# All units of an attention and maxout kernel queued in another order

## The chip, the cores and the metric

The kernel runs on one core of one Trainium2 chip. The metric is the device time of one execution in microseconds (us): the median of the runs, beside the time of one execution under the profiler.

## The reference

Four sequences of 768 tokens, 8 heads of 64. Each query sees the first 8 positions (at a fixed distance) and the last 96, with a bias that falls with distance at a slope of its own for each head. The heads' outputs stand side by side as 3072 rows of 512 and go through a network whose hidden layer is the maximum of three products.

```python
scores = scale * np.matmul(q, k.transpose(0, 1, 3, 2))
keep = is_global | is_local          # pos < 8, or 0 <= rel < 96
dist = np.where(is_global & ~is_local, float(n_local), np.abs(rel))
scores = np.where(keep, scores - slopes[:, None, None] * dist, -1e9)
a = softmax(scores)                  # over the keys
x = np.matmul(a, v)                  # to (3072, 512)
h = np.maximum(np.maximum(x @ w1, x @ w2), x @ w3)    # 512 -> 768
return h @ w_out                     # 768 -> 512
```

## The kernel before, in words

The work is cut into units, each a small function, and a string SCHEDULE lists 504 of them. A loop at the end of the kernel calls them in that order, and every engine then runs its own instructions strictly in that order: a unit that waits holds all that stands behind it on its engine. SP issues nearly all DMAs, in the same order. Within one unit, TensorE, ACT, VectorE, GpSimd and SP only wait for one another where data or a buffer ties them.

A unit is a letter and numbers. T is a token tile of 128 tokens (0 to 23, six to a sequence), n is a part of two tiles (0 to 11). The last number often names the engine of the copy: 0 ACT, 1 VectorE, 2 GpSimd.

- l n.s loads queries (s = 0) or keys (s = 1) of part n (load_part, tile rawp; l0.1 goes by ACT's queue, the others by SP's), c n.s.how casts them to bf16 (cast_part, tile qkp), x n.s.how transposes them into qkT: on TensorE through PSUM (how 2 and 3 in whole tiles with one copy of 1024 columns; 6, 7, 8 in halves with two copies: one on each engine, both on ACT, both on VectorE), or by a DMA on SP (9).
- v n loads values, C n.e.how casts half of them into vo (the first part of a sequence into vof), Y n.half.how copies rows of vo into ve or vf, which hold the same values at another shift; V T.how and G T.how write the 8 global values and keys in their place, Z b.how gathers the first keys of a sequence into kf.
- B h.how and K h make the bias and the mask of head h from the distances (tiles bias, wmask).
- S T.g.how are the scores of four heads (PSUM tile sp) and their exponential on ACT (tile P). With how 1 the bias is added on TensorE by two matmuls with the identity; with how 0 M T.g multiplies P by wmask on VectorE later.
- A T.how multiplies by the values (PSUM op; with 2, two smaller tiles oph) and normalises on VectorE (tile xb); T T.how transposes the result into xT: on TensorE, copied by ACT (0, 7), VectorE (1, 8) or both (6), or by a DMA on SP (4).
- w, o load weights, W, Q cast them. F c.f.j is one of the three products of hidden block f in chunk c: four matmuls into PSUM h (line 424), then for j = 0 a copy on ACT (429), for j = 1 and 2 a maximum on VectorE (431, 433). Chunks hold 4, 2, 2, 4, 4, 4, 4 token tiles; chunks 1 and 2 are of half width. O c.tt.how is the output of one token tile: six matmuls (439), a copy (448) and a store. E is the last chunk's, in pieces.
- D i.n is n filler matmuls (line 504, tile wp), whose result is not used.

PSUM sets limits to the order: three rotating buffers (h) for F, O, the filler and half the transposes, one buffer (tp) for the other transposes, and two (sp0, sp1) for S and A. Loads have 5 buffers for queries and keys and 3 for values.

Of the kernel before, what the change touches and what calls it, by code (L numbers as in the profile page):

```python
# [22 lines left out]


SCHEDULE = """
    K7 l1.0 c1.0.2 K6 l1.1 B6.1 D0.6 D4.4 B5.1 D2.0 D5.4 K0 c0.1.1 c0.0.1 K2 D8.0 B0.1 B4.0 B1.0
    B3.0 x0.1.3 K1 K3 K5 c1.1.2 B7.0 x0.0.7 D1.1 D9.2 S1.0.1 Z0.1 B2.1 v0 C0.0.2 S1.1.1 G1.0 x1.0.8
    K4 M1.0 S0.0.1 M0.0 v1 x1.1.8 S2.1.1 S2.0.1 M2.0 C0.1.2 Y0.1.2 Y1.0.1 M1.1 V2.1 Y0.0.1 G2.1 A1.2
    S0.1.1 C1.0.2 C1.1.2 Y2.0.0 Y1.1.2 D3.1 S3.0.1 M3.0 M0.1 A0.2 S3.1.1 M3.1 l2.0 c2.0.2 x2.0.6
    T1.1 M2.1 A2.0 V3.2 T0.0 G3.0 A3.1 l2.1 c2.1.2 x2.1.6 T2.1 w0.0 W0.0.0 l3.0 w0.1 S4.0.1 M4.0  # L30
    T3.8 V4.2 W0.1.2 S4.1.0 D7.1 G4.0 w0.2 F0.1.0 F0.0.0 S5.1.0 c3.0.1 x3.0.6 M4.1 w1.0 W1.0.0
    S5.0.0 F0.1.1 W0.2.2 F0.1.2 v2 C2.0.0 C2.1.0 W2.0.1 F0.0.1 F0.0.2 M5.0 F0.3.0 F0.2.0 M5.1 Y2.1.1
    V5.1 F0.5.0 w1.1 W1.1.0 W2.1.1 F0.4.0 A4.1 A5.0 F0.5.1 T4.0 F0.4.1 w1.2 W1.2.0 l3.1 T5.1 F0.2.1
    F0.2.2 l4.0 c4.0.1 W2.2.0 F0.5.2 c3.1.0 x3.1.7 Z1.0 F0.4.2 F1.0.0 F1.2.0 l4.1 c4.1.1 S7.0.0
    S6.1.0 l5.0 x4.0.6 l5.1 o0 F1.0.1 F1.0.2 c5.0.1 M7.0 F1.3.0 F1.4.0 F1.4.1 o2 c5.1.1 x4.1.7
    S6.0.0 S7.1.0 G7.0 v3 F1.2.1 F1.2.2 F1.3.1 Q2.1 F0.3.1 M7.1 Q0.0 F1.5.0 F1.5.1 S8.0.0 x5.0.7
    S8.1.0 G8.1 C3.0.2 C3.1.1 Y4.0.1 F0.3.2 F1.5.2 A7.0 F1.4.2 F1.1.0 M6.0 x5.1.6 v5 o1 Q1.0 v4
    S9.0.0 S9.1.0 l7.0 l6.1 C5.0.1 C5.1.0 F1.1.1 F1.3.2 Y3.1.1 M8.0 F1.1.2 T7.0 v6 l6.0 M6.1 v7
    Y3.0.1 M9.0 O0.2.1 l7.1 C4.0.0 O0.0.0 G9.0 V8.1 A6.1 c7.0.1 M8.1 c6.1.1 x6.1.9 O0.3.0 C4.1.0
    Y4.1.1 O0.1.1 Y5.1.0 S10.1.0 T6.8 V9.1 M9.1 S10.0.0 O1.0.0 A8.1 M10.1 T8.4 F2.0.0 x7.0.9 G10.0  # L40
    F2.4.0 c6.0.0 l8.1 v9 l9.1 F2.0.1 F2.1.0 M10.0 F2.0.2 S11.0.0 c7.1.0 Y5.0.1 x6.0.6 S11.1.0 V10.1
    F2.1.1 M11.0 F2.4.1 C6.0.0 A9.0 F2.2.0 V11.1 l9.0 O1.1.1 S13.1.0 x7.1.6 S13.0.0 G13.0 M11.1
    F2.2.1 F2.1.2 C6.1.1 F2.2.2 A11.1 F2.3.0 F2.5.0 A10.0 Y6.1.0 Z2.0 F2.4.2 T11.0 F2.5.1 F2.3.1
    C7.0.0 S12.1.0 T9.8 S12.0.0 F2.3.2 v8 C7.1.1 F2.5.2 M12.0 S14.1.0 T10.6 S14.0.0 c8.1.0 O2.0.0
    l8.0 M13.0 G14.1 Y7.1.1 M12.1 F3.2.0 V15.0 M13.1 c9.1.1 x9.1.9 F3.0.0 Y7.0.1 A13.1 F3.3.0 l11.1
    T13.4 M14.0 x8.1.9 M14.1 F3.0.1 S15.1.0 Y6.0.0 S15.0.0 F3.3.1 F3.3.2 F3.1.0 M15.0 M15.1 V14.0
    F3.4.0 c8.0.1 c9.0.0 x9.0.9 l10.0 F3.0.2 A12.1 F3.2.1 x8.0.9 C9.0.0 C8.0.0 A14.0 F3.1.1 T12.4
    l10.1 G15.1 Y8.0.1 c11.1.0 O2.1.0 A15.1 F3.5.0 F3.1.2 C9.1.1 F3.2.2 T15.8 S19.0.0 M19.0 S19.1.0
    c10.0.0 T14.4 C8.1.0 Y8.1.0 F3.4.1 l11.0 v10 F3.5.1 F3.5.2 F3.4.2 Y10.0.1 M19.1 Z3.1 S16.0.0
    S16.1.0 G16.1 V20.0 O3.3.0 O3.2.1 A19.1 F4.5.0 c10.1.1 x10.1.9 v11 F4.1.0 V16.1 G19.1 x10.0.9  # L50
    Y9.0.1 S18.1.0 S17.0.0 M17.0 M16.1 F4.3.0 F4.3.1 F4.5.1 M16.0 V17.1 F4.1.1 S17.1.0 S18.0.0
    F4.2.0 Y9.1.0 O3.0.0 M18.0 M17.1 C10.0.1 M18.1 A16.1 F4.1.2 T19.4 O3.1.1 A18.0 A17.1 C11.0.1
    c11.0.0 x11.0.9 F4.0.0 F4.2.1 F4.2.2 F4.3.2 T18.4 S20.1.0 S20.0.0 T16.4 T17.4 x11.1.9 C10.1.1
    Y10.1.1 F4.0.1 G20.1 F4.0.2 F4.5.2 S21.0.0 S21.1.0 G21.0 M20.0 F4.4.0 F4.4.1 C11.1.1 F4.4.2
    M21.1 F5.1.0 F5.2.0 V21.1 O4.2.1 F5.3.0 Y11.1.0 F5.3.1 M20.1 S22.0.0 S22.1.0 F5.2.1 F5.5.0
    Y11.0.0 F5.2.2 V23.1 F5.4.0 A20.1 F5.3.2 M22.0 M21.0 G22.0 S23.0.0 M23.0 S23.1.0 T20.4 F5.5.1
    O4.1.1 A21.1 T21.4 M23.1 M22.1 O4.0.0 V22.0 F5.4.1 F5.0.0 A23.1 T23.4 O4.3.0 A22.0 F5.4.2 F5.5.2
    F5.0.1 F5.1.1 F5.0.2 T22.4 F5.1.2 F6.3.0 F6.5.0 F6.4.0 F6.5.1 F6.4.1 F6.4.2 O5.1.0 F6.3.1 F6.1.0
    O5.3.1 F6.1.1 F6.0.0 F6.0.1 F6.0.2 O5.0.1 F6.2.0 F6.2.1 F6.3.2 O5.2.0 F6.2.2 F6.1.2 F6.5.2 E
    D6.0  # L60
"""


# [510 lines left out]
```

## Time and profile before

| | us |
|---|---|
| median of 3 runs | 176.2 (176.19 to 176.25) |
| the profiled execution, its own time | 176.69 |
| span of that execution in the trace | 174.9 |
| TensorE busy | 168.4 |
| VectorE busy | 133.0 |
| ACT busy | 120.1 |
| GpSimd busy | 14.0 |

The times of rows are those of the profiled execution, from the start of its span. A timeline row gives start, length, engine, line, operation, tiles and count, and in brackets how long the engine was idle and what ended that. Where a row merges several instructions, its length runs from the first start to the last end; spacings of starts are shorter than lengths, since the instructions of an engine overlap a little. A line number is that of the kernel before; the changed kernel's lines from 57 on are one lower, because its SCHEDULE has one line less.

### The profile page before, as it was taken

The numbers are of one execution on the slowest core, as the hardware profiler recorded it, in microseconds if no ns is written. First come the engines' busy times: TensorE is split into PE (matmuls) and PEld (weight loads), VectorE is DVE, ScalarE is ACT, GpSimd is POOL, SyncE is SP. The second block draws the span as 40 slices with busy tenths as digits, with TensorE's granted clock in tenths as the row PEclk, the third lists the DMA queues.
The fourth block names the chain that finished last, engine by engine and source line by source line (L and its number), as shares of the span: only waits on it lengthen the run. The fifth ranks groups of instructions, "written<-read, shape, count | busy, mean of one in ns | idle before, by whom it ended". The sixth has DMA issues, their size and how long they took to land.

```text
span 174.9 us, 4215 instructions
## 1 busy us (share of the span) xinstructions
PE 168.4 (96%) x1664; PEld 92.8 (53%) x1685; DVE 133.0 (76%) x287; ACT 120.1 (69%) x188; POOL 14.0 (8%) x25
## 2 busy tenths in 40 slices
...
GB/s 130 350 301 334 363 350 381 384 335 325 317 275 278 324 280 223 291 219 211 219 226 216 285 208 177 166 133 60 56 8 30 108 168 0 0 119 36 88 27 213
DMA packets 55508, 35.92 MB, mean 205 GB/s; under 512 B 18369, under 2 KB 47937, under 8 KB 55489
## 3 DMA queue, kind: packets, MB, share of 16 engines
...
q8 instruction: 13, 0.21, 0.5%
...
## 4 chain that ended last, share of the span: by engine, by line
PE 88%; ACT 5%; DVE 3%; issue 2%; POOL 1%; POOLq 0%; ACTq 0%
PE h L424 52%; PE po L439 18%; PE sp L306 7%; PE op L360 5%; ACT wmask L326 2%; PE tpr L261 2%; PE sp L299 2%; ACT bias L322 1%; ACT qkT L268 1%; PE xtp L411 1%; ACT P L317 1%; POOL qkp L188 1%; PE oph L360 1%; PE xtr L401 0%; DVE xb L373 0%
## 5 line engine op out<-in xcount | busy, mean ns | idle before, releaser
L424 PE MATMUL h<-xT,w 128*128 128x512 bf16 (+1 forms) x489 | 99.5, 348 | 0.9 <-issue 0.3
L424 PEld LDWEIGHTS <-w 128*128 128x128 bf16 x504 | 46.6, 98 | 41.0 <-ACT w L493 1.1
L317 ACT ACTIVATE P<-sp 128x1024 bf16<-128x1024 f32 (+1 forms) x48 | 44.0, 956 | 9.2 <-PE sp L306 9.1
L429 ACT CAST h<-h 128x512 bf16<-128x512 f32 (+1 forms) x42 | 21.8, 531 | 21.9 <-PE h L424 21.8
L439 PE MATMUL po<-wo,ht 128*128 128x512 bf16 (+2 forms) x150 | 33.8, 362 | 0.4
L431 DVE TENSOR_TENSOR h<-h,h 128x512 bf16<-128x512 bf16 (+1 forms) x42 | 25.2, 605 | 10.9 <-PE h L424 8.9
L433 DVE TENSOR_TENSOR ht<-h,h 128x512 bf16<-128x512 bf16 (+1 forms) x42 | 25.5, 608 | 6.7 <-PE h L424 5.0
L334 DVE TENSOR_TENSOR P<-P,wmask 128x1024 bf16<-128x1024 bf16 x33 | 22.4, 696 | 2.0 <-ACT P L317 1.9
L439 PEld LDWEIGHTS <-ht 128*128 128x128 bf16 x156 | 14.4, 98 | 15.0 <-DVE ht L433 0.2
L448 ACT COPY ost<-po 128x512 f32<-128x512 f32 (+2 forms) x16 | 8.8, 554 | 15.8 <-PE po L439 15.3
L373 DVE TENSOR_TENSOR xb<-op,rz 128x512 bf16<-128x512 f32 x22 | 15.2, 692 | 0.8
L360 PEld LDWEIGHTS <-P 128*128 128x128 bf16 x352 | 13.4, 97 | 4.0 <-issue 0.2
L306 PE MATMUL sp<-qkT 64*128 64x128 bf16 x320 | 14.3, 217 | 0.2
L306 PEld LDWEIGHTS <-qkT 64*128 64x128 bf16 x320 | 9.3, 94 | 8.4 <-issue 5.1
L448 DVE COPY ost<-po 128x512 f32<-128x512 f32 (+1 forms) x10 | 6.5, 648 | 8.4 <-PE po L439 8.4
L188 DVE CAST qkp<-rawp 128x1024 bf16<-128x1024 f32 x12 | 8.2, 687 | 2.0 <-DMA rawp<-in_k_dram 1.8
L188 ACT CAST qkp<-rawp 128x1024 bf16<-128x1024 f32 x8 | 8.4, 1050 | 0.0
L504 PE MATMUL wp<-const-bfloat16-1.0 128*128 128x512 bf16 x19 | 7.5, 539 | 0.9 <-PEq L555 0.8
L268 ACT COPY qkT<-tpr 128x512 bf16<-128x512 bf16 x12 | 6.6, 588 | 1.0 <-PE tpr L261 1.0
L268 DVE COPY qkT<-tpr 128x512 bf16<-128x512 bf16 x6 | 4.0, 688 | 3.6 <-PE tpr L261 3.6
L261 PE MATMUL tpr<-identb,qkp 64*128 64x64 bf16 x208 | 5.4, 190 | 0.6 <-DVE qkp L188 0.2
L493 ACT CAST w<-wst 128x1024 bf16<-128x1024 f32 x5 | 5.1, 1047 | 1.0 <-DMA wst<-in_moe_w_dram 1.0
...
## 6 DMA issues: line engine op xcount, KB each, us to landing
...
```

The lines of the kernel that those rows point to most:

```text
L188: copies[how](qk, src)
L306: nc.tensor.matmul(sp[:, z, i, ds], k_cols(T, hsl, jp, ds), q_cols(T, hsl, jp), start=not how, stop=True, skip_group_check=True)
L317: nc.scalar.activation(dst, src, AF.Exp, bias=0.0, scale=scale)
L334: nc.vector.tensor_mul(P, P, wmask[:, g, :, 0:2])
L360: nc.tensor.matmul(o, P[:, i, ds], vs[ds][:, h], start=(ds == 0), stop=(ds == len(vs) - 1), skip_group_check=True)
L373: nc.vector.tensor_tensor(out=x.rearrange("p (g h) d -> p g h d", g=2), in0=o4[:, :, :, 0:64], in1=rz[:, :, :, None].to_broadcast([128, 2, ...
L424: nc.tensor.matmul(ps, w123[f // 2][:, dm, j, (f % 2) * 128:(f % 2) * 128 + 128], xT[c][:, dm], start=(dm == order[0]), stop=(dm == order[ ...
L429: nc.scalar.copy(h01, ps)
L431: nc.vector.tensor_max(h01s[c, f], h01s[c, f], ps)
L433: nc.vector.tensor_max(ht[c][:, f], h01s[c, f], ps)
L439: nc.tensor.matmul(po, ht[c][:, f, tt * 128:(tt + 1) * 128], wo[:, f, cols], start=(f == 0), stop=(f == NF - 1))
L448: copy(ost, po)
```

## The change

Only SCHEDULE differs: 500 units instead of 504, all in another order, and for many the engine of a copy. Work is the same but for this: S4.0 takes mask M4.0 and no bias matmuls; A16 and A20 are split in two PSUM tiles; T9 and T15 go by DMA; x3.1 and x1.1 are transposed in whole tiles now, x0.1 in halves; ten D units have become six, and the filler is 19 matmuls in both, of which one (D9.1) now stands behind E. Summed over the program the ACT copies of O go from 11 to 16, the VectorE casts c from 12 to 15, the GpSimd casts C from 5 to 2 (C0.0, C0.1 and C1.0 go to VectorE, Y0.0 and V2 to GpSimd). The first line of the string, before and now, and the units up to F0.1.0, now:

```diff
-    K7 l1.0 c1.0.2 K6 l1.1 B6.1 D0.6 D4.4 B5.1 D2.0 D5.4 K0 c0.1.1 c0.0.1 K2 D8.0 B0.1 B4.0 B1.0
...
+    K4 B3.1 K3 c0.0.2 B0.1 B4.1 K6 B6.2 K1 K0 K7 B1.0 B2.1 K2 B7.0 D7.3 D3.3 D0.8 c0.1.1 K5 x0.1.8
+    B5.0 l1.1 c1.1.0 D8.2 x0.0.6 D4.2 S1.0.1 l1.0 c1.0.1 M1.0 Z0.1 S1.1.1 M1.1 x1.1.3 v0 C0.0.1 G1.0
...
```

GpSimd, from its first cast to its last two casts of weights. Before:

```order
L188 CAST qkp<-rawp 128x1024 x2
L191 CAST vof_107<-rawv 128x8x64 x2
L195 COPY vf_113<-vof_107 64x260
L191 CAST vo_109<-rawv 128x8x64 x2
L195 COPY ve_111<-vo_109 64x520
L188 CAST qkp<-rawp 128x1024
L195 COPY vo_109<-vof_107 4x520
L188 CAST qkp<-rawp 128x1024
L195 COPY ve_112<-vof_107 4x520
L493 CAST w_0_116<-wst 128x4x256 x2
```

And now:

```order
L187 CAST qkp<-rawp 128x1024
L321 TENSOR_SCALAR bias<-rbq 128x384
L194 COPY vf_113<-vof_107 64x260 x2
L194 COPY ve_111<-vof_107 4x520
L190 CAST vo_109<-rawv 128x8x64
L194 COPY ve_111<-vo_109 64x520
L187 CAST qkp<-rawp 128x1024
L194 COPY vo_109<-vof_107 4x520
L187 CAST qkp<-rawp 128x1024
L492 CAST w_0_116<-wst 128x4x256 x2
```

The casts at its head were c1.0 and c1.1 and are c0.0 alone; bias B6 has come, three casts of values have left, and the last copy (V4) has left. The casts in the middle were c2.0, c2.1 and are c2.1, c2.0; the weights were W0.1, W0.2 and are W0.0, W0.2.

ACT, from the last wmask ahead of the first exponential to the first exponentials of token tiles 0 and 2. Before:

```order
L326 ACTIVATE wmask<-rbq 128x384 x3
L322 ACTIVATE bias<-rbq 128x384
L268 COPY qkT<-tpr 128x8x64 x2
L317 ACTIVATE P<-sp 128x1024 x2
L233 COPY qkT<-qkT 128x8x4
L326 ACTIVATE wmask<-rbq 128x384
L317 ACTIVATE P<-sp 128x4x128
L317 ACTIVATE P<-sp 128x1024 x2
```

And now:

```order
L325 ACTIVATE wmask<-rbq 128x384
L321 ACTIVATE bias<-rbq 128x384
L187 CAST qkp<-rawp 128x1024
L267 COPY qkT<-tpr 128x8x64
L316 ACTIVATE P<-sp 128x1024 x2
L232 COPY qkT<-qkT 128x8x4
L267 COPY qkT<-tpr 128x8x64
L316 ACTIVATE P<-sp 128x4x128
L316 ACTIVATE P<-sp 128x1024 x2
```

The last wmask (K4) has moved ahead of the first exponential, a cast (c1.1) has come before it, and one copy of x1.0 stands behind it.

SP, the first loads. Before:

```order
L168 DMA rawp<-in_q_dram 128x1x512 x4
L164 DMA rawp<-in_k_dram 128x8x128
L175 DMA rawv<-in_v_dram 128x8x128 x2
L168 DMA rawp<-in_q_dram 128x1x512 x2
L164 DMA rawp<-in_k_dram 128x8x128
L483 DMA wst<-in_moe_w_dram 128x4x256
L168 DMA rawp<-in_q_dram 128x1x512 x2
L483 DMA wst<-in_moe_w_dram 128x4x256 x2
L483 DMA wst<-in_moe_w_dram 128x4x512
```

And now:

```order
L167 DMA rawp<-in_q_dram 128x1x512 x2
L163 DMA rawp<-in_k_dram 128x8x128
L167 DMA rawp<-in_q_dram 128x1x512 x2
L174 DMA rawv<-in_v_dram 128x8x128 x2
L163 DMA rawp<-in_k_dram 128x8x128
L167 DMA rawp<-in_q_dram 128x1x512 x2
L482 DMA wst<-in_moe_w_dram 128x4x256 x3
L482 DMA wst<-in_moe_w_dram 128x4x512
```

Keys now stand ahead of queries in parts 1 and 2 (a part's queries are two loads of half the size), and l3.0 is no longer between the weights.

More of the change, by code (lines that the diff above doesn't have):

```diff
@@ L25 @@
 SCHEDULE = """
-    K7 l1.0 c1.0.2 K6 l1.1 B6.1 D0.6 D4.4 B5.1 D2.0 D5.4 K0 c0.1.1 c0.0.1 K2 D8.0 B0.1 B4.0 B1.0
[L27 to L60, printed above, removed]
+    K4 B3.1 K3 c0.0.2 B0.1 B4.1 K6 B6.2 K1 K0 K7 B1.0 B2.1 K2 B7.0 D7.3 D3.3 D0.8 c0.1.1 K5 x0.1.8
@@ new lines @@
+    B5.0 l1.1 c1.1.0 D8.2 x0.0.6 D4.2 S1.0.1 l1.0 c1.0.1 M1.0 Z0.1 S1.1.1 M1.1 x1.1.3 v0 C0.0.1 G1.0
+    C0.1.1 x1.0.6 S0.0.1 M0.0 S2.1.1 v1 C1.0.1 Y0.1.2 Y0.0.2 Y1.0.1 V2.2 S2.0.1 G2.0 C1.1.2 A1.2
+    Y1.1.2 l2.1 S0.1.1 S3.0.1 M3.0 c2.1.2 V3.2 M2.0 M0.1 A0.2 S3.1.1 G3.0 M3.1 M2.1 A2.0 l2.0 x2.1.7
+    c2.0.2 w0.0 T0.1 W0.0.2 w0.1 A3.1 T2.0 x2.0.6 T1.0 T3.1 S4.1.0 Y2.0.1 S4.0.0 G4.1 F0.1.0 F0.0.0
+    S5.1.0 W0.1.1 w0.2 S5.0.0 M4.1 F0.0.1 w1.0 W2.0.0 W1.0.0 M5.1 v2 F0.1.1 W0.2.2 C2.1.0 F0.0.2
@@ new lines @@
+    C2.0.0 F0.1.2 M5.0 Y2.1.1 F0.5.0 M4.0 V5.0 w1.1 F0.4.0 F0.3.0 V4.1 W1.1.1 F0.2.0 W2.1.0 A5.1
+    A4.0 F0.3.1 F0.2.1 w1.2 W2.2.1 l3.1 F0.5.1 W1.2.0 T5.0 F0.4.1 c3.1.0 T4.0 F0.5.2 x3.1.2 l3.0
+    c3.0.1 F0.3.2 l4.1 c4.1.1 F1.2.0 F1.2.1 Z1.0 x3.0.7 l4.0 c4.0.1 F0.4.2 F1.4.0 S7.1.0 x4.0.6
+    S7.0.0 F1.4.1 F1.2.2 v3 C3.1.1 F1.1.0 l5.0 c5.0.1 G7.1 F1.1.1 S6.1.0 M6.1 Y3.1.1 x4.1.7 S6.0.0
+    F0.2.2 F1.0.0 M7.0 x5.0.7 S8.1.0 M7.1 S8.0.0 G8.0 F1.1.2 F1.4.2 C3.0.2 F1.0.1 F1.5.0 Y3.0.1 o2
+    l5.1 c5.1.1 A7.1 F1.3.0 F1.3.1 o0 Q0.1 F1.5.1 o1 Q1.1 Q2.0 M6.0 x5.1.7 S9.1.0 v4 S9.0.0 G9.0
@@ new lines @@
+    C4.1.0 M8.1 F1.0.2 T7.1 C4.0.0 F1.3.2 l6.1 v5 l7.0 l6.0 l7.1 l8.0 O0.2.0 A6.1 Y4.0.1 V8.1 O0.3.0
+    c6.1.1 x6.1.9 M9.0 M8.0 O0.0.0 T6.6 v6 S10.1.0 S10.0.0 G10.1 Y5.0.1 Y4.1.1 F1.5.2 M10.1 V9.1
+    O0.1.0 c7.0.1 M10.0 A8.1 T8.4 F2.1.0 F2.5.0 C5.0.1 x7.0.9 F2.4.0 F2.0.0 c6.0.0 F2.0.1 F2.4.1
+    F2.5.1 M9.1 S11.1.0 c7.1.0 S11.0.0 x6.0.6 F2.1.1 F2.5.2 C5.1.1 A9.1 T9.4 F2.3.0 Y5.1.1 M11.0
+    M11.1 O1.0.0 F2.3.1 F2.3.2 S13.0.0 S13.1.0 C6.0.0 x7.1.6 V10.1 v7 v9 F2.0.2 V11.1 Z2.0 F2.1.2
+    F2.2.0 G13.1 A10.0 A11.1 O1.1.1 T10.6 S12.0.0 S12.1.0 M13.0 F2.4.2 F2.2.1 C6.1.1 c8.0.1 v8 l9.0
```

16 lines of the change are left out of this document (added).

## The prediction, as it was made before the run

> **What bounds the kernel now.** I read the page's busy shares first, then the chain that ended last, then each engine's timeline.
>
> ```profile
> span 174.9 us, 4215 instructions
> PE 168.4 (96%) x1664; PEld 92.8 (53%) x1685; DVE 133.0 (76%) x287; ACT 120.1 (69%) x188; POOL 14.0 (8%) x25
> PE 88%; ACT 5%; DVE 3%; issue 2%; POOL 1%; POOLq 0%; ACTq 0%
> ```
>
> TensorE is busy 96% of the span and carries 88% of the chain. A busy PE may still be waiting, so I look at its timeline (start, length, engine, line, tiles, count).
>
> ```profile
> 21.14 0.39 PE L504 MATMUL wp<-const-bfloat16-1.0 128*128 128x512 bf16 x1
> 21.56 1.89 PE L424 MATMUL h<-xT,w 128*128 128x512 bf16 x7
> 24.17 7.25 PE L424 MATMUL h<-xT,w 128*128 128x512 bf16 x31
> 140.24 10.53 PE L424 MATMUL h<-xT,w 128*128 128x512 bf16 x47
> 166.15 5.37 PE L439 MATMUL po<-wo,ht 128*128 128x512 bf16 x35
> ```
>
> The row of 47 matmuls holds 48 (F1 units have four each; one record is missing): 10.53 / 48 = 0.219 us a matmul. From F0.1.0 (21.56) on PE has 360 wide F1 matmuls (78.8 us), 144 of half the width (15.8), 144 of O and E (31.5) and, by my count of the small rows, some 15 us of scores, values and transposes: 141. They took until 166.15 + 5.37 = 171.5, that is 150. Most of the difference is spread over a hundred changes from one kind of matmul to another, which any order has. I estimate what a better order could still win there at 1 us. So PE is saturated behind 21.56, and what stands ahead of it is a start-up of 21.56 us in which PE does filler (the wp row at 21.14 is its last) and small work for ACT, VectorE, GpSimd and the loads. **The start is the term to work out; the rest can mostly be lost.**
>
> What sets the start is seen on ACT and GpSimd.
>
> ```profile
> 3.11 2.09 ACT L326 ACTIVATE wmask<-rbq 128x384 bf16<-128x384 f32 x4 [0.43 <-DVE rbq L529]
> 5.11 1.33 ACT L322 ACTIVATE bias<-rbq 128x384 bf16<-128x384 f32 x3
> 8.26 1.04 ACT L268 COPY qkT<-tpr 128x512 bf16<-128x512 bf16 x2
> 9.79 1.94 ACT L317 ACTIVATE P<-sp 128x1024 bf16<-128x1024 f32 x2 [0.49 <-PE sp L306]
> 20.29 1.05 ACT L493 CAST w<-wst 128x1024 bf16<-128x1024 f32 x1
> 21.24 1.94 ACT L317 ACTIVATE P<-sp 128x1024 bf16<-128x1024 f32 x2
> ```
> ```profile
> 8.09 1.04 POOL L188 CAST qkp<-rawp 128x1024 bf16<-128x1024 f32 x1 [4.92 <-DMA rawp<-in_q_dram]
> 9.80 1.04 POOL L188 CAST qkp<-rawp 128x1024 bf16<-128x1024 f32 x1 [0.68 <-DMA rawp<-in_k_dram]
> 12.85 0.40 POOL L195 COPY vf<-vof 64x260 int32<-64x260 int32 x1
> L191 POOL CAST vof<-rawv 128x512 bf16<-128x512 f32 x3 | 1.8, 616 | 21.7 <-DMA rawv<-in_v_dram 20.9 <-DVE qkT L268 0.8
> 13.46 1.59 POOL L191 CAST vo<-rawv 128x512 bf16<-128x512 f32 x2 [0.21 <-DMA rawv<-in_v_dram]
> 15.11 0.61 POOL L195 COPY ve<-vo 64x520 int32<-64x520 int32 x1
> 15.79 1.04 POOL L188 CAST qkp<-rawp 128x1024 bf16<-128x1024 f32 x1
> 18.28 1.04 POOL L188 CAST qkp<-rawp 128x1024 bf16<-128x1024 f32 x1 [0.89 <-PE op L360]
> 22.46 1.04 POOL L493 CAST w<-wst 128x1024 bf16<-128x1024 f32 x1 [2.58 <-DMA wst<-in_moe_w_dram]
> ```
>
> (One row gives a group over the whole span: its busy time, then 616 ns as the mean of one.) ACT runs almost without a gap from 3.11. The exponentials of token tile 4, the last ahead of F0, end at 21.24 + 1.94 = 23.18. GpSimd's cast at 18.28 (c2.1) is late because its keys land late:
>
> ```profile
> L164 SPq DMA_DIRECT2D rawp<-in_k_dram x1: 457/457/457, 10.4 to 10.4; - x1
> DMA to landing us min/median/max: 7.8/7.8/7.8
> ```
>
> 10.4 + 7.8 = 18.2 us, the landing of l2.1.
>
> **The change, part by part.** *ACT up to the first exponential.* Spacings: 0.52 for a wmask (2.09 by 4), 0.41 for a bias (1.24 until the next row, by 3), 0.97 for a wide exponential or a 1024-column cast, 0.5 for a copy. Before, 7 wmask, 4 bias and 2 copies end at 9.3, and 0.49 is waited. Now 8 wmask (4.2; K4 comes ahead), 3 bias (1.2), the cast c1.1 (1.0) and one copy (0.5) make 6.9: 3.11 + 6.9 = 10.0. The first exponential goes from 9.79 to 10.0, **+0.2**. PE has S1.0 ready at about 9.6, since it needs only GpSimd's c0.0, the transposes and VectorE's half of the copies; c0.0's data are the first two loads of SP:
>
> ```profile
> L168 SPq DMA_DIRECT2D rawp<-in_q_dram x2: 577/618/659, 0.7 to 1.5; - x2
> DMA to landing us min/median/max: 5.1/5.2/5.2
> ```
>
> 1.5 + 5.1 = 6.6, and the cast is done at 7.65.
>
> *ACT from there to the end of tile 4's exponentials.* Before 13.4 us. Now 8 wide exponentials (7.8), 2 narrow (1.0), 3 short copies G (0.4), 6 copies from PSUM (3.0), and by my walk 0.2 of waiting: 12.4. K4 (0.5), the values' copy Y2.0 (1.0) and the cast W0.0 (1.0) have left this stretch, and more PSUM copies have come. 10.0 + 12.4 = 22.4 against 23.18: **-0.8**.
>
> *GpSimd.* Its chain is now Y0.1, Y0.0, V2, C1.1, Y1.1, c2.1, V3, c2.0, W0.0. It starts when VectorE has cast C0.0 and C0.1 (12.7, after c1.0, Z0.1 and x1.1): 0.40 + 0.40 = 13.5; V2 waits for VectorE's Y1.0 (14.4), then 0.61, 0.61, 0.61 bring 16.25; c2.1 1.04 = 17.3; V3 0.61; c2.0 1.04 = 18.95; W0.0 waits for its load:
>
> ```profile
> L483 SPq DMA_DIRECT2D wst<-in_moe_w_dram x1: 1109/1109/1109, 10.9 to 10.9; - x1
> DMA to landing us min/median/max: 8.7/8.7/8.7
> ```
>
> 10.9 + 8.7 = 19.6 (the same bytes stand ahead of it now), plus 1.04 = 20.65. The bias B6 on GpSimd is not in the trace: below nothing excluded, at most a 1024-column cast's 1.04; I take 0.5 by the 0.61 of a 512-column cast, and S1.1 needs it only at 9.6, so both ends cost nothing.
>
> *What opens F0.1.0.* W0.0 at 20.65 (GpSimd), T1.0's copy at 20.65 (ACT), T3.1's copy at 20.7 (VectorE: A3's result at 19.7, a copy of x2.0 0.6, its own 0.4). Three engines arrive together; F0.1.0 starts near 20.75 instead of 21.56: **-0.8**. The two bias matmuls of S4.0 (0.4 on PE, ahead of this point) go too, inside it.
>
> *VectorE beside GpSimd.* One copy of before shows what stands to be lost or saved:
>
> ```profile
> 8.24 1.02 DVE L208 COPY kf<-qkT 128x512 bf16<-128x512 bf16 x1
> L208 DVE COPY kf<-qkT 128x512 bf16<-128x512 bf16 x2 | 1.3, 654 | 0.0
> ```
>
> The copy of 1.02 us ran beside GpSimd's cast of 8.09 and ended 0.13 us behind it; its twin later took 1.31 - 1.02 = 0.29. The sum uses 0.29 for Z0.1, which now has no GpSimd work beside it. One collision is left by my walk: C1.0 on VectorE (the second values land at 13.4, where GpSimd's cast of 13.46 waited for them) beside Y0.0 until 13.5, price 0.15, already in. The Trainium skill, page "SBUF — State Buffer", section "Who interferes with whom", says that a VectorE copy in a two-port mode and a GpSimd instruction lock one pair of ports against each other for the whole instruction; the row agrees, as the copy ended right behind the cast. By the same rule VectorE's W0.1 and the mask M4.1 could wait for GpSimd's W0.0 or W0.2, by up to 1.04 each; VectorE's next customer F0.0.1 leaves PE at 23.9 and hides that.
>
> *Loads.* l3.0 moves behind the weights, so w0.1 to w1.2 come about one 512 KB load earlier. GpSimd's rows of 8.09 and 9.80 waited for two loads in succession, 1.7 apart: I take 1.4 and bound it by 0 and 1.8.
>
> ```profile
> 26.69 1.04 ACT L493 CAST w<-wst 128x1024 bf16<-128x1024 f32 x1 [1.03 <-DMA wst<-in_moe_w_dram]
> ```
>
> w1.0 landed at 26.7 and should land at 25.3; W2.0 then starts on ACT when its exponentials end, 25.35, and F0.5.0 follows F0.1.2 at 26.5 without a wait. In before these waits (1.03 here, 2.58 above) cost PE little: 7.25 us for 32 matmuls, 0.24 over 32 x 0.219. So the gain is 0 to 0.24 and I take 0.
>
> *The rest.* Counted over the whole program, VectorE loses about 1 us (five stores' copies less, two PE transposes' copies moved to DMA, against three casts, one mask and two split normalisations more), ACT loses about 1, PE gains or loses nothing beyond 0.3. D9.1, one filler matmul (0.39 in the row of 21.14), stands behind PE's last useful matmul, covered by the last copies and stores; without that cover it would cost 0.4. T and x that go by DMA are queued on SP behind stores; the nearest case, x9.1 to S19, has nine F1 units between, 36 x 0.219 = 7.9 us.
>
> *Sum.* Start -0.8, F0's loads 0, later order 0 with bounds -1.0 and +2.0 (below). The profiled execution took 176.69 (span 174.9 and 1.8 around it): 175.9. The median of the runs is 0.49 under it: 176.2 - 0.8 = **175.4**.
>
> **The rivals.** *(1) VectorE becomes the bound, slower.* The windows (length, PE, PEld, DVE, ACT, POOL, then clock and DMA):
>
> ```profile
> 50.00:60.00 10.00, 9.88 (x109) 5.67 (x105) 9.86 (x24) 9.12 (x15) 0.00 (x0) 1.00 1.09 288
> 60.00:70.00 10.00, 9.95 (x168) 8.03 (x168) 9.87 (x25) 9.78 (x17) 0.00 (x0) 1.00 1.27 261
> ```
>
> ```profile
> 65.84 0.40 DVE L431 TENSOR_TENSOR h<-h,h 128x256 bf16<-128x256 bf16 x1
> 66.17 0.19 DVE L372 RECIPROCAL rz<-op 128x8 f32<-128x8 f32 x1
> 66.39 0.69 DVE L373 TENSOR_TENSOR xb<-op,rz 128x512 bf16<-128x512 f32 x1
> 67.00 0.41 DVE L195 COPY vo<-vof 4x520 int32<-4x520 int32 x1
> 67.34 0.67 DVE L448 COPY ost<-po 128x512 f32<-128x512 f32 x1
> 67.94 0.40 DVE L266 COPY qkT<-tpr 128x512 bf16<-128x512 bf16 x1
> ```
>
> VectorE is over 98% busy there while PE still runs dense. At the spacings of these starts, 0.60 (store copy; mask, wide maximum and cast are as long), 0.33 (narrow maximum), 0.34 (values' copy) and 0.83 (a normalisation), the stretch from the first O0 unit to the first F3 units holds 23.5 us of VectorE work before and 26.6 now, for about 26 of PE. For it: 26.6 is more than 26. Against: in the stretch ahead VectorE has 1.7 less, and its largest backlog against PE, summed unit by unit, is 2.4 to 2.9 us now and was 2.9 to 3.3 before, without a stall. It decides once VectorE's spacing is over 5% above those figures; then 28.1 against 26 costs 2.0, less what is hidden in the 0.3 to 0.5 of old gaps: -0.8 + 1.5 = +0.7, **176.9**. *(2) The keys of l2.1 land no earlier (18.2)*, though they stand one load ahead: c2.1 ends 19.25, PE's transposes 19.65, ACT waits 1.45: F0.1.0 at 22.1, +0.5, of which the earlier weights return some 0.1: **176.6**. Against: the queries that had this place were cast at 15.79 without a wait. *(3) The start's gain is given back*, because w1.0 lands no earlier (26.7): W2.0 is ready at 27.7 where PE wants it at 26.5, or GpSimd's chain is held by collisions of the same size: **176.2**, no change. *(4) The later order saves its share too* (small gaps of 0.2 to 0.6 at a dozen F1 and O rows): -0.8 - 0.8: **174.6**.
>
> **How the numbers follow.** Forecast (175.0 to 175.8) 0.42, (4) 0.13, (3) 0.13, (1) 0.22, (2) 0.10. A measurement of this kernel tells about 0.2%, 0.35 us, from no change. Faster 0.42 + 0.13 = 0.55; same 0.13; slower 0.32. Range: down to 174.2, where the bound of 1.0 is nearly reached, up to 177.0, which takes in (1) and (2); the bound of +2.0 without any gain behind it is left out.
>
> **What would show it.** The first h row on PE near 20.75; tile 4's exponentials ending near 22.4 on ACT; GpSimd's W0.0 behind its load with no row longer than its kind; no VectorE copy over 0.45 us at 12 to 15 us. Then PE from F0.1.0 to its last matmul as long as before (150 us). Wrong would be: c2.1 at 18 us or later, a wait of PE for w near 26, or a PE stretch between 47 and 80 us with gaps beyond 1 us while VectorE has no idle.

## The result, and the profile after

The changed kernel took 175.34 us (median of 6 runs, 175.29 to 175.45) against 176.22 for the kernel before (6 runs, 176.19 to 176.55): a ratio of 0.9947 with a 95% interval of 0.9934 to 0.996, 0.9 us less. The profiled execution took 175.30, so here profile and median agree. The page of the changed kernel, answering to the first fence of the prediction:

```profile
span 173.5 us, 4167 instructions
PE 168.0 (97%) x1636; PEld 93.0 (54%) x1659; DVE 130.2 (75%) x285; ACT 119.6 (69%) x192; POOL 12.4 (7%) x23
PE 77%; DVE 12%; ACT 7%; issue 2%; POOL 0%; POOLq 0%; ACTq 0%; DVEq 0%
```

TensorE's busy time is 168.0 where it was 168.4, while the span lost 1.4. A few matmul records are missing in both; in a second profile of each (below), where none is missing, it is 168.9 now and 168.7 before, and the span is 1.2 shorter. So the time came out of places where TensorE had nothing to run, not out of TensorE's work. Its timeline in the changed kernel (start, length, engine, line, tiles, count):

```profile
20.85 1.89 PE L423 MATMUL h<-xT,w 128*128 128x512 bf16 x7
23.22 7.08 PE L423 MATMUL h<-xT,w 128*128 128x512 bf16 x31
30.14 0.65 PE L359 MATMUL op<-vo,P 128*128 128x65 bf16 x16
163.59 6.67 PE L438 MATMUL po<-wo,ht 128*128 128x512 bf16 x42
170.10 0.38 PE L503 MATMUL wp<-const-bfloat16-1.0 128*128 128x512 bf16 x1
```

The first h row, F0.1.0, begins at 20.85 where it began at 21.56. The second holds F0's next eight units, up to the first op row: 32 matmuls (one record is missing) in 7.08 us instead of 7.25. The last useful matmul ends at 163.59 + 6.67 = 170.26 instead of 171.52. From F0.1.0 to there TensorE took 149.4 us, where it took 150.0. The single wp row at 170.10 is D9.1.

ACT in the changed kernel:

```profile
8.36 1.03 ACT L187 CAST qkp<-rawp 128x1024 bf16<-128x1024 f32 x1
9.77 1.92 ACT L316 ACTIVATE P<-sp 128x1024 bf16<-128x1024 f32 x2
15.89 2.14 ACT L316 ACTIVATE P<-sp 128x1024 bf16<-128x1024 f32 x2 [0.47 <-PE sp L305]
20.71 1.94 ACT L316 ACTIVATE P<-sp 128x1024 bf16<-128x1024 f32 x2
25.30 2.03 ACT L492 CAST w<-wst 128x1024 bf16<-128x1024 f32 x2
```

The first exponential is where it was (9.77 against 9.79); tile 4's end at 22.65 instead of 23.18. The last row is the two casts of the weights w1.0 (W2.0 and W1.0), with no idle time in brackets: ACT takes them up at 25.30, as soon as it is free, and so w1.0 has landed by then. Before, it was waited for until 26.69. The load's own row, from its issue at 13.6, says the same:

```profile
L482 SPq DMA_DIRECT2D wst<-in_moe_w_dram x1: 1060/1060/1060, 13.6 to 13.6; - x1
DMA to landing us min/median/max: 11.5/11.5/11.5
```

13.6 + 11.5 = 25.1 us.

GpSimd in the changed kernel:

```profile
7.73 1.17 POOL L321 TENSOR_SCALAR bias<-rbq 128x384 bf16<-128x384 f32 x1
14.23 0.61 POOL L194 COPY ve<-vof 4x520 int32<-4x520 int32 x1 [0.95 <-DVE ve L194]
16.14 1.04 POOL L187 CAST qkp<-rawp 128x1024 bf16<-128x1024 f32 x1
17.98 1.03 POOL L187 CAST qkp<-rawp 128x1024 bf16<-128x1024 f32 x1 [0.24 <-PE tpr L260]
19.39 1.04 POOL L492 CAST w<-wst 128x1024 bf16<-128x1024 f32 x1 [0.38 <-DMA wst<-in_moe_w_dram]
```

These are B6, V2, c2.1, c2.0 and W0.0. In the kernel before, the last of these casts of queries and keys was c2.1, at 18.28 behind its load; now both c2.1 and c2.0 are done by 19.0, and W0.0 follows its own load.

**How to find where a gain sits.** The orders of the two kernels differ, so equal times on the clock do not mean equal work. I therefore ask of a unit how late it is: its start, less the TensorE work that stands ahead of it since F0.1.0, each kind of matmul counted at its regular spacing (0.217 us for a 512-column one). Example: the first op row behind F0 starts at 30.14 in the changed kernel; 40 wide matmuls (8.68) and two score units (0.55) stand ahead, so it is late by 30.14 - 9.23 = 20.91 (20.93 in the table, which uses the spacings unrounded): nearly what F0.1.0 was, so F0 lost next to nothing. Two further profiled executions of the kernel before (below) are the more usual ones and stand in the table.

| | F0.1.0 | first A in F0 | first O0 | last A | end of the last useful matmul |
|---|---|---|---|---|---|
| before, first profile | 21.56 | 21.81 | 22.87 | 24.66 | 171.52 |
| before, two later profiles | 21.33 and 21.34 | 21.73 | 22.70 | 24.48 | 171.33 |
| changed | 20.85 | 20.93 | 21.71 | 23.48 | 170.26 |

Against the usual profile of before: the start gives 0.48; F0 loses 0.08 where it lost 0.40, which gives 0.32; from there to O0 0.78 is lost where it was 0.97, which gives 0.19. From O0 to the last A the two lose 1.77 and 1.78, so in sum nothing behind 50 us differs. Together 1.0, and 1.07 at the last matmul; by the medians it is 0.88.

### The profile page after: what moved, and what is told of

It is laid out like the page before. It is cut to its first block, busy times and chain, and to the rows that moved or that the text cites. A ratio compares the mean times of both kernels' runs of the same rounds, so it can differ in the third digit from the quotient of the medians.

```text
span 173.5 us, 4167 instructions
## 1 busy us (share of the span) xinstructions
PE 168.0 (97%) x1636; PEld 93.0 (54%) x1659; DVE 130.2 (75%) x285; ACT 119.6 (69%) x192; POOL 12.4 (7%) x23
## 4 chain that ended last, share of the span: by engine, by line
PE 77%; DVE 12%; ACT 7%; issue 2%; POOL 0%; POOLq 0%; ACTq 0%; DVEq 0%
PE h L423 50%; PE po L438 14%; PE sp L305 5%; PE op L359 4%; ACT P L316 3%; DVE P L333 3%; ACT wmask L325 2%; DVE h L430 1%; DVE ve L194 1%; DVE xb L372 1%; PE tpr L260 1%; DVE qkp L187 1%; PE xtp L410 1%; DVE ht L432 1%; ACT bias L321 1%
## 5 line engine op out<-in xcount | busy, mean ns | idle before, releaser
L428 ACT CAST h<-h 128x512 bf16<-128x512 f32 (+1 forms) x42 | 21.6, 537 | 26.5 <-PE h L423 26.0
L438 PE MATMUL po<-wo,ht 128*128 128x512 bf16 (+2 forms) x147 | 33.1, 362 | 0.5
L432 DVE TENSOR_TENSOR ht<-h,h 128x512 bf16<-128x512 bf16 (+1 forms) x42 | 25.3, 607 | 3.1 <-PE h L423 2.0
L447 ACT COPY ost<-po 128x512 f32<-128x512 f32 (+2 forms) x21 | 11.7, 566 | 13.9 <-PE po L438 13.4
L359 PEld LDWEIGHTS <-P 128*128 128x128 bf16 x352 | 12.9, 97 | 3.8 <-ACT P L316 0.4
L372 DVE TENSOR_TENSOR xb<-op,rz 128x512 bf16<-128x512 f32 x20 | 13.8, 691 | 0.7
L305 PE MATMUL sp<-qkT 64*128 64x128 bf16 x320 | 13.1, 217 | 0.0
L187 DVE CAST qkp<-rawp 128x1024 bf16<-128x1024 f32 x15 | 10.2, 681 | 2.1 <-DMA rawp<-in_k_dram 1.3
L447 DVE COPY ost<-po 128x512 f32<-128x512 f32 (+1 forms) x5 | 3.0, 607 | 6.1 <-PE po L438 6.1
L190 ACT CAST vo<-rawv 128x512 bf16<-128x512 f32 x11 | 6.6, 638 | 0.0
L187 ACT CAST qkp<-rawp 128x1024 bf16<-128x1024 f32 x6 | 6.2, 1042 | 0.0
L371 DVE RECIPROCAL rz<-op 128x8 f32<-128x8 f32 x20 | 4.0, 198 | 1.7 <-PE op L359 1.7
L359 PE MATMUL op<-vo,P 128*128 128x65 bf16 x128 | 5.2, 193 | 0.0
## 6 DMA issues: line engine op xcount, KB each, us to landing
wst<-in_moe_w_dram SPq DMA_DIRECT2D x3, 1024.0 KB, 11.5
```

The lines of the kernel that those rows point to most:

```text
L187: copies[how](qk, src)
L305: nc.tensor.matmul(sp[:, z, i, ds], k_cols(T, hsl, jp, ds), q_cols(T, hsl, jp), start=not how, stop=True, skip_group_check=True)
L359: nc.tensor.matmul(o, P[:, i, ds], vs[ds][:, h], start=(ds == 0), stop=(ds == len(vs) - 1), skip_group_check=True)
L372: nc.vector.tensor_tensor(out=x.rearrange("p (g h) d -> p g h d", g=2), in0=o4[:, :, :, 0:64], in1=rz[:, :, :, None].to_broadcast([128, 2, ...
L428: nc.scalar.copy(h01, ps)
L432: nc.vector.tensor_max(ht[c][:, f], h01s[c, f], ps)
```

## The experiments

Kernels of one group ran on one chip beside runs of the kernel before. The first group holds the next three kernels and one repeat of the kernel before (median of the runs beside them 176.21), the second the four from "The load l3.0 alone put back" to "A cast from ACT to GpSimd" (176.26), the third the one without two filler matmuls and one repeat of each of the two kernels (176.30). Their line numbers are two lower than those of before.

### The changed start alone

The changed order up to F0.1.0, with l3.0 put back between the weights, then the order of before. Against the changed kernel:

```diff
-    c2.0.2 w0.0 T0.1 W0.0.2 w0.1 A3.1 T2.0 x2.0.6 T1.0 T3.1 S4.1.0 Y2.0.1 S4.0.0 G4.1 F0.1.0 F0.0.0
-    S5.1.0 W0.1.1 w0.2 S5.0.0 M4.1 F0.0.1 w1.0 W2.0.0 W1.0.0 M5.1 v2 F0.1.1 W0.2.2 C2.1.0 F0.0.2
+    c2.0.2 w0.0 l3.0 T0.1 W0.0.2 w0.1 A3.1 T2.0 x2.0.6 T1.0 T3.1 S4.1.0 Y2.0.1 S4.0.0 G4.1 V4.2 W0.1.2 w0.2
+    F0.1.0 F0.0.0 S5.1.0 c3.0.1 x3.0.6 M4.1 M4.0 w1.0 W1.0.0 S5.0.0 F0.1.1 W0.2.2 F0.1.2 v2 C2.0.0
...
```

> The changed order up to F0.1.0, then the order of before (with its loads: l3.0 between w0.0 and w0.1). Theory, the start is the gain: F0.1.0 begins at 20.8 to 20.9 and the kernel takes 175.4 to 175.6, most of the changed kernel's 175.3. Rival, the gain comes from the order and the loads behind F0.1.0: 176.0 to 176.2 whatever the start.

Measured: 176.29, ratio 1.0003 (0.9994 to 1.0011). TensorE and ACT of this kernel:

```profile
20.86 1.89 PE L422 MATMUL h<-xT,w 128*128 128x512 bf16 x7
23.47 7.48 PE L422 MATMUL h<-xT,w 128*128 128x512 bf16 x31
```
```profile
26.10 1.05 ACT L491 CAST w<-wst 128x1024 bf16<-128x1024 f32 x1 [1.06 <-DMA wst<-in_moe_w_dram]
```

F0.1.0 is as early as in the changed kernel, and still the time is that of before. F0 loses 0.49 now (the first A is late by 21.35), because ACT waits 1.06 for w1.0; its next 32 matmuls take 7.48 us, where the changed kernel has 7.08. From there to O0 0.97 is lost, as in before. Its last useful matmul ends at 171.08, 0.25 ahead of the usual profile of before; in the medians nothing is left of that. My theory that the start carries the gain by itself is refuted.

### The later order alone

The order of before up to F0.1.0, then the changed order (less V4.1, W0.1.1, l3.0 and w0.2, which have been done by then; S4.0 keeps its bias on TensorE, so M4.0 has nothing to do):

```diff
-    S4.1.0 D7.1 G4.0 w0.2 F0.1.0 F0.0.0 S5.1.0 c3.0.1 x3.0.6 M4.1 w1.0 W1.0.0 S5.0.0 F0.1.1 W0.2.2 F0.1.2
+    S4.1.0 D7.1 G4.0 w0.2 F0.1.0 F0.0.0 S5.1.0 S5.0.0 M4.1 F0.0.1 w1.0 W2.0.0 W1.0.0 M5.1 v2 F0.1.1 W0.2.2
...
```

> The order of before up to F0.1.0, then the changed order (with the loads of before up to w0.2). Theory, the start is the gain: F0.1.0 at 21.5 to 21.6 and 175.8 to 176.2, a gain of at most 0.4 from the order behind it. Rival, the later order is the gain: 175.3 to 175.5.

Measured: 176.56, ratio 1.0014 (1.0005 to 1.0023): slower than before, which neither side had expected. The rows of this kernel:

```profile
21.34 1.89 PE L422 MATMUL h<-xT,w 128*128 128x512 bf16 x7
23.71 7.37 PE L422 MATMUL h<-xT,w 128*128 128x512 bf16 x31
```
```profile
26.35 1.99 ACT L491 CAST w<-wst 128x1024 bf16<-128x1024 f32 x2 [0.47 <-DMA wst<-in_moe_w_dram]
```
```profile
116.78 0.62 PE L304 MATMUL sp<-qkT 64*128 64x128 bf16 x16 [0.24 <-PE h L422]
```

F0 again loses 0.44 (21.34 to 21.78). From the first A to O0 it loses 0.78 as the changed kernel does, so the 0.19 saved there belongs to the later order; but behind O0 it loses 2.24 up to its last A (22.56 to 24.80), 0.5 more than the others. More than half of the 0.5 is one stop, the row of 116.78 (S21.1 and S21.0), which comes 0.30 later behind the unit ahead of it than in the changed kernel. Why it waits there, and where the rest is lost, was not traced. Start and later order, each put alone, give nothing.

### The values' copies alone put back

Here the three casts of values go back to GpSimd and the two copies to VectorE, and the order stays that of the changed kernel.

```diff
-    C0.0.1 G1.0 C0.1.1
-    S2.1.1 v1 C1.0.1 Y0.1.2 Y0.0.2 Y1.0.1 V2.2
+    C0.0.2 G1.0 C0.1.2
+    S2.1.1 v1 C1.0.2 Y0.1.2 Y0.0.1 Y1.0.1 V2.1
```

> The changed kernel with C0.0, C0.1 and C1.0 back on GpSimd and Y0.0 and V2 back on VectorE, order unchanged. Theory, three engines share the start and GpSimd's chain has some 0.4 us to spare ahead of c2.1: 175.3 to 175.7, VectorE copies of 0.6 us or more beside GpSimd at 12 to 15 us. Rival, the values' move off the collisions is the gain: F0.1.0 at 21.4 or later and 176.0.

Measured: 175.44, ratio 0.995 (0.9937 to 0.9964), 0.1 from the changed kernel and inside its interval. VectorE's row in this kernel, then GpSimd's, then ACT's:

```profile
12.46 0.67 DVE L193 COPY vf<-vof 64x260 int32<-64x260 int32 x1 [0.23 <-POOL vof L189]
```
```profile
13.62 0.89 POOL L189 CAST vo<-rawv 128x512 bf16<-128x512 f32 x1 [0.64 <-DVE ve L193]
16.40 1.04 POOL L186 CAST qkp<-rawp 128x1024 bf16<-128x1024 f32 x1
```
```profile
8.59 1.05 ACT L186 CAST qkp<-rawp 128x1024 bf16<-128x1024 f32 x1
```

The collisions are there: a 260-column copy on VectorE takes 0.67, where the median of its five copies of this kind in this kernel is 0.29, and a 512-column cast 0.89 where the mean of its group was 0.616 in before. The Trainium skill, page "SBUF — State Buffer", section "Who interferes with whom", gives the reason, a pair of ports that VectorE and GpSimd lock against each other; the rows agree with it. But they cost next to nothing at the end: c2.1 starts at 16.40 instead of 16.14, and F0.1.0 at 21.12 instead of 20.85, and in this execution 0.23 of that was already there in ACT's cast of 8.59 (8.36 in the changed kernel), ahead of any value. By the medians, what the copies' new engine is worth is about 0.1, and not to be told from nothing.

### The load l3.0 alone put back

The changed kernel, with l3.0 again between w0.0 and w0.1:

```diff
-    c2.0.2 w0.0 T0.1 W0.0.2 w0.1
+    c2.0.2 w0.0 l3.0 T0.1 W0.0.2 w0.1
...
-    x3.1.2 l3.0 c3.0.1
+    x3.1.2 c3.0.1
```

> The changed kernel with the load l3.0 alone put back between w0.0 and w0.1. Theory, the later loads carry about 0.3 us of the gain: F0.1.0 still at 20.85, PE's row of F1 matmuls behind it 0.2 to 0.4 longer, 175.6 to 175.8. Rival, the loads' order is without effect and only the start and the engines' shares count: 175.3 to 175.4.

Measured: 176.05, ratio 0.9989 (0.998 to 0.9998). One moved load gives back 0.71 of the 0.88, about twice what was expected of it. TensorE and ACT of this kernel:

```profile
20.85 1.89 PE L422 MATMUL h<-xT,w 128*128 128x512 bf16 x8
23.23 3.63 PE L422 MATMUL h<-xT,w 128*128 128x512 bf16 x16
27.75 3.63 PE L422 MATMUL h<-xT,w 128*128 128x512 bf16 x16 [0.89 <-ACT w L491]
31.28 0.64 PE L358 MATMUL op<-vo,P 128*128 128x65 bf16 x16
```
```profile
26.64 1.99 ACT L491 CAST w<-wst 128x1024 bf16<-128x1024 f32 x2 [1.18 <-DMA wst<-in_moe_w_dram]
```

The start is that of the changed kernel to a hundredth. Then w1.0 is taken up at 26.64 instead of 25.30, ACT waits 1.18 for it, and TensorE stands 0.89 in front of F0.5.0: the op row starts at 31.28 instead of 30.14, 1.14 late. Those 1.14 stay to the end (last useful matmul at 171.41 against 170.26). This profiled execution took 176.46, 0.41 above the median of its kernel, so in most runs the load's loss is smaller, about 0.7. (In the kernel with the changed start alone w1.0 came at 26.10 with the same loads ahead of it; such a difference between two executions is about that 0.41.)

### The load moved in the kernel before

The opposite edit: in the order of before l3.0 goes behind l3.1, and its cast and transposes behind those of l3.1.

```diff
-    w0.0 W0.0.0 l3.0 w0.1 S4.0.1 M4.0
+    w0.0 W0.0.0 w0.1 S4.0.1 M4.0
...
-    S5.1.0 c3.0.1 x3.0.6 M4.1 w1.0
+    S5.1.0 M4.1 w1.0
...
-    w1.2 W1.2.0 l3.1 T5.1
+    w1.2 W1.2.0 l3.1 l3.0 T5.1
...
-    c3.1.0 x3.1.7 Z1.0
+    c3.1.0 x3.1.7 c3.0.1 x3.0.6 Z1.0
```

> The kernel before with l3.0 behind l3.1, and its cast c3.0 and transposes x3.0 behind x3.1. Theory: F0.1.0 as before, the F1 matmuls behind it without a wait for w, 175.8 to 176.0. Rival, without the earlier start the loads hide nothing: 176.2.

Measured: 177.91, ratio 1.0091 (1.0078 to 1.0105), 1.7 us slower, outside both expectations. TensorE and VectorE:

```profile
36.45 0.41 PE L259 MATMUL tpr<-identb,qkp 64*128 64x64 bf16 x16
38.45 0.41 PE L259 MATMUL tpr<-identb,qkp 64*128 64x64 bf16 x16 [1.59 <-DVE qkp L186]
```
```profile
37.70 0.69 DVE L186 CAST qkp<-rawp 128x1024 bf16<-128x1024 f32 x1
```

F0 does gain (the first A is late by 21.41 instead of 21.73: the 0.32 of the changed kernel). But x3.0 (the row of 38.45) now stands right behind x3.1 (that of 36.45), and TensorE waits 1.59 for its cast, which begins only at 37.70. TensorE at the same place in the changed kernel:

```profile
35.87 0.61 PE L281 MATMUL tpp<-identb,qkp 128*128 128x128 bf16 x8
36.31 1.90 PE L423 MATMUL h<-xT,w 128*128 128x512 bf16 x12
38.15 0.41 PE L260 MATMUL tpr<-identb,qkp 64*128 64x64 bf16 x16
```

There x3.0 comes no earlier (38.15), but F0.3.2, F1.2.0 and F1.2.1, 1.90 us of matmuls, stand between it and x3.1. So the move pays only where the order behind it has work to put in front of x3.0.

### Start and load together, with the later order of before

```diff
-    c2.0.2 w0.0 l3.0 T0.1 W0.0.2 w0.1
+    c2.0.2 w0.0 T0.1 W0.0.2 w0.1
...
-    S5.1.0 c3.0.1 x3.0.6 M4.1 M4.0 w1.0
+    S5.1.0 M4.1 M4.0 w1.0
...
-    w1.2 W1.2.0 l3.1 T5.1
+    w1.2 W1.2.0 l3.1 l3.0 T5.1
...
-    c3.1.0 x3.1.7 Z1.0
+    c3.1.0 x3.1.7 c3.0.1 x3.0.6 Z1.0
```

(against the kernel with the changed start alone).

> The changed order up to F0.1.0, the order of before behind it, and l3.0, c3.0 and x3.0 late. Theory, start and loads together are the gain and each alone is lost in the other's wait: 175.4 to 175.7. Rival, the order of the units behind F0 is needed for it: 176.0 to 176.2.

Measured: 178.11, ratio 1.0096 (1.0081 to 1.0112), outside both expectations. The transposes x3.0 of this kernel:

```profile
38.32 0.41 PE L259 MATMUL tpr<-identb,qkp 64*128 64x64 bf16 x16 [1.84 <-DVE qkp L186]
```

F0.1.0 starts at 20.90 and the first A of F0 is late by 21.04, so 0.69 is won there against the usual profile of before; at O0 it is late by 24.28, 2.57 more than the changed kernel. Start and load do what they should; then 3.24 are lost up to O0 where before loses 0.97, and these 2.3 are over three times what was won. 1.84 of them is TensorE's wait for x3.0, as in the kernel above.

### A cast from ACT to GpSimd

In the changed kernel the cast c1.1 stands on ACT in front of the first exponential. If ACT sets the start, taking it off must bring F0.1.0 forward.

```diff
-    B2.1 K2 B7.0 D7.3 D3.3 D0.8 c0.1.1 K5 x0.1.8 B5.0
-    l1.1 c1.1.0 D8.2 x0.0.6
+    B2.1 B5.1 K2 B7.0 D7.3 D3.3 D0.8 c0.1.1 K5 x0.1.8
+    l1.1 c1.1.2 D8.2 x0.0.6
```

(B5 goes from ACT to VectorE as well.)

> The changed kernel with the cast c1.1 on GpSimd instead of ACT and the bias B5 on VectorE, early. ACT has 1.3 us less ahead of the first exponential. Theory, ACT sets the start: the first exponential at 9.45 instead of 9.77, F0.1.0 at 20.6 to 20.75, 175.1 to 175.25. Rival, GpSimd's chain up to c2.0 sets it (19.0, then the transposes x2.0): F0.1.0 at 20.85, 175.3 to 175.4.

Measured: 175.24, ratio 0.9939 (0.9927 to 0.9951). TensorE, ACT and VectorE of this kernel:

```profile
20.64 1.89 PE L422 MATMUL h<-xT,w 128*128 128x512 bf16 x8
```
```profile
8.19 0.58 ACT L266 COPY qkT<-tpr 128x512 bf16<-128x512 bf16 x1
9.50 1.94 ACT L315 ACTIVATE P<-sp 128x1024 bf16<-128x1024 f32 x2 [0.73 <-PE sp L304]
```
```profile
9.78 0.81 DVE L186 CAST qkp<-rawp 128x1024 bf16<-128x1024 f32 x1 [0.86 <-DMA rawp<-in_q_dram]
```

ACT's work ahead of the first exponential shrank by the cast's 1.03 and a bias's 0.41, but the exponential came only 0.27 earlier (9.50), because it then waits 0.73 for TensorE's scores behind the last copy (8.19). F0.1.0 starts 0.21 earlier and the last useful matmul ends 0.20 earlier (170.06). The medians differ by 0.1 and the two intervals overlap, so the step is shown by the traces, not by the times. VectorE's cast of 0.81 lies beside GpSimd's new one and is slower than c3.0's 0.69 above, without effect on the end.

### The same without two filler matmuls

D4.2, which stands ahead of the first scores, is left out: its two filler matmuls are not computed.

```diff
-    l1.1 c1.1.2 D8.2 x0.0.6 D4.2 S1.0.1
+    l1.1 c1.1.2 D8.2 x0.0.6 S1.0.1
```

> The changed kernel with c1.1 on GpSimd, B5 on VectorE, and the filler D4.2 between the first transposes and the first scores left out (its two matmuls' result is not used). Theory: the scores of S1.0 then wait for VectorE's copy alone, the first exponential starts at 9.4 instead of 9.5 and F0.1.0 at 20.55: 175.1 to 175.2. Rival: the filler kept the granted clock up or filled a wait, 175.25 or more.

Measured: 175.12, ratio 0.9929 (0.9905 to 0.9952), the fastest of all, though its interval holds that of the kernel above. The first exponential in this kernel:

```profile
9.42 1.94 ACT L315 ACTIVATE P<-sp 128x1024 bf16<-128x1024 f32 x2 [0.63 <-PE sp L304]
```

It starts 0.08 earlier, and F0.1.0 0.01 (20.63, not the 20.55 expected). The granted clock of the profiled execution is 1.0 with and without these two matmuls.

### The two kernels again

The kernel before was run again twice and the changed one once, with no edit, to see how much of a profile is the execution and how much the kernel.

> The kernel before once more, for a second profile: the first one took 176.69 where the runs' median is 176.2. Theory: 176.2, F0.1.0 at 21.5, and the missing 0.5 us stands in one place of the trace. Rival: 176.7 with the profile as before, the profile itself costs 0.5.

> The kernel before, for another profile. Theory, its executions differ in the start: one of 176.2 has F0.1.0 near 21.1 and the same time behind it as the profiles of 176.5 and 176.7. Rival: F0.1.0 at 21.3 and 0.3 us less behind it.

> The changed kernel again, beside e9 on one chip. Theory: 175.3, e9 0.1 to 0.2 under it. Rival: no difference that can be told.

Measured: before, one profiled execution of 176.48 with F0.1.0 at 21.33, where 176.2 and 21.5 were expected; before again, median 176.19 of 12 runs, ratio 0.9992 (0.9978 to 1.0006), its profiled execution 176.50; changed, 175.33, ratio 0.9944 (0.9926 to 0.9963), its profiled execution 175.32 with F0.1.0 at 20.86. GpSimd's, ACT's and TensorE's rows of the last profile of before:

```profile
17.23 1.03 POOL L186 CAST qkp<-rawp 128x1024 bf16<-128x1024 f32 x1
```
```profile
26.60 1.04 ACT L491 CAST w<-wst 128x1024 bf16<-128x1024 f32 x1 [1.15 <-DMA wst<-in_moe_w_dram]
```
```profile
21.34 1.89 PE L422 MATMUL h<-xT,w 128*128 128x512 bf16 x8
23.95 7.38 PE L422 MATMUL h<-xT,w 128*128 128x512 bf16 x32
165.96 5.37 PE L437 MATMUL po<-wo,ht 128*128 128x512 bf16 x36
```

Here c2.1 starts at 17.23 with no wait for its keys; in the profile of the prediction it started at 18.28 after 0.89 of idle time. So the late landing of l2.1, on which I had built a part of the start, belonged to that execution. The wait for w1.0 is in all three, and with the earlier start of F0 it weighs more here: the 32 matmuls take 7.38 us, not 7.25. All three profiled executions of before lie 0.3 to 0.5 above its median, those of the changed kernel do not; of the 12 runs ten took 176.17 to 176.28 and two 176.50 and 176.58. Which wait is shorter in the usual runs is not in any trace, and it stays open; so about 0.3 us of what the traces divide up between start, load and order is not in the medians.

## Why the prediction was right, and which steps were not

The time was forecast at 175.4 and came out at 175.34, faster, inside the range. The way there was right in part.

- **First exponential, +0.2.** It did not move (9.77). ACT was full up to it as described, with the cast c1.1 until 8.36 + 1.03 = 9.39 and one copy behind it; the walk had ACT full until 10.0 and was 0.2 too long.
- **End of tile 4's exponentials, -0.8.** 22.65, that is -0.5. The stretch was 12.9 us long, not 12.4. The walk had 0.2 of waiting in it; ahead of the row of 15.89 alone ACT waited 0.47.
- **GpSimd.** c2.1 to about 17.2, c2.0 to 19.0, W0.0 19.39 to 20.43: forecast 17.3, 18.95 and 20.65. Here the walk was right to 0.2. B6 took 1.17, above the bound of 1.04 that I had put to it, and was hidden as the prediction said.
- **F0.1.0, -0.8.** It started at 20.85, forecast 20.75. The three engines did arrive nearly together: W0.0 ended at 20.43, T1.0's copy at 20.65 and T3.1's at 20.70. But the 21.56 it was set against came from an execution with late keys; against 21.34 the start is worth 0.5.
- **VectorE beside GpSimd.** No copy of values took over 0.45 at 12 to 15 us. (One copy of x1.0, at 12.20, took 0.68, and 0.688 is the mean of its kind in the kernel before: the sign was put too widely.) VectorE's cast C1.0 shows nothing of the 0.15 priced in, since GpSimd's copies end at 12.43 + 0.85 = 13.28, just as it begins:

```profile
12.43 0.85 POOL L194 COPY vf<-vof 64x260 int32<-64x260 int32 x2 [3.53 <-DVE vof L190]
13.28 0.43 DVE L190 CAST vo<-rawv 128x512 bf16<-128x512 f32 x1 [0.40 <-DMA rawv<-in_v_dram]
13.74 0.43 DVE L194 COPY ve<-vof 64x520 int32<-64x520 int32 x1
```

  Putting the values' copies back brought the collisions back and cost at most 0.1. So this part of the change is not where its gain is.
- **Loads, taken at 0 out of 0 to 0.24. This is the step that failed, by its size.** That w1.0 would be there at 25.3 was right (ACT's row of 25.30 has no wait). I read the price of the wait in before off the length of one row, 7.25 us for 32 matmuls, as if the earlier start would not change it. But the earlier F0 starts, the earlier it wants w1.0; with the load left where it was, the loss is 1.14 in the trace and 0.7 in the medians. That is rival (3), which I had priced at 27.7 - 26.5 = 1.2 and given 0.13. Its price and place were right. It did not come about because w1.0 did land earlier (25.1), and without that most of the gain would not have reached the end. The load's term is -0.32 in the trace of the changed kernel against before, and -0.7 against the changed kernel without it.
- **Later order, 0.** From O0 on right. Between F0 and O0 it gave 0.19. Beyond that it has a part the prediction did not see: it gives x3.0 a place where its late load costs nothing (1.59 us of waiting at the other place). That TensorE would take 150 us from F0.1.0 on, as before, was 0.5 too long: it took 149.4, less by this 0.19 and the load's 0.32.
- **Rival (1), VectorE as the bound.** Windows of the changed kernel (length, PE, PEld, DVE, ACT, POOL, clock, DMA):

```profile
50.00:60.00 10.00, 9.89 (x103) 6.49 (x106) 9.84 (x23) 8.98 (x17) 0.00 (x0) 1.00 1.18 274
60.00:70.00 10.00, 9.65 (x163) 7.81 (x163) 9.75 (x27) 8.91 (x15) 0.00 (x0) 1.00 1.07 221
70.00:80.00 10.00, 9.95 (x113) 5.61 (x113) 9.09 (x21) 7.92 (x17) 0.00 (x0) 1.00 0.93 248
```
```profile
67.25 1.56 PE L423 MATMUL h<-xT,w 128*128 128x256 bf16 x12 [0.24 <-DVE h L430]
```

  VectorE is no fuller than before, and from O0 to the last A both kernels lose the same (1.77 and 1.78). The price of the rival did not come about. Its mechanism came near, though: the chain on the page has 12% on VectorE, 3% before, most of it in one piece from 47.0 to 67.2 us, and at its end TensorE waits 0.24 for VectorE's maximum, where before has no such wait. In the second profile of the changed kernel the wait is 0.25 and the chain has 5% on VectorE, so in this stretch the two engines are about equally full.
- **Rival (2), keys no earlier.** c2.1 at 16.14 refutes it.

The sum: forecast -0.8, all from the start; measured about -0.5 from the start, -0.3 from w1.0 and -0.2 ahead of O0, 1.0 in the traces and 0.88 in the medians. Two errors offset: a start taken too large by an unusual profile, and loads taken too small. That the forecast came within 0.1 is partly luck. The sum also hides that the parts, each put into the kernel before, do not add up: the start alone changes nothing (176.29), the later order alone costs 0.3, the load alone 1.7, start and load 1.9, and all together save 0.9.

In one order of steps they do add up. The later order alone took 176.56; with the new start as well, which is the changed kernel with l3.0 alone put back, 176.05; with the load moved as well 175.34. Behind the later order the start is thus worth 0.5 and the load 0.7, after a loss of 0.35. (The first two ran on different chips, beside 176.21 and 176.26, and differ in four small units around F0.1.0 too.)
